# A fused attention and GeGLU kernel: a planner decides the order of work, a quarter of the softmax exponentials is computed on VectorE, and the softmax is normalised with queries on partitions

## The chip, the cores and the metric

The kernel runs on one core of one Trainium2 chip. The metric is the device time of one execution in microseconds, lower is better. Each kernel was run several times; a time "854.13 (853.46 to 855.33)" is the median and the range. A profile is one of these executions; its span is about 2 us shorter than the time of the same run.

Engines are named as in the profile: PE is TensorE's matmuls, PEld its weight loads, DVE is VectorE, ACT is ScalarE, POOL is GpSimd, SP is SyncE.

## The reference

```
x: 2048 tokens x 640;  H = 32 heads of Dh = 20;  Df = 1536          (bf16)
h  = x + Attention(layernorm(x))     # one k and one v head (20 wide) for all 32 query heads
     q = xn @ wq (2048 x 640),  k = xn @ wk,  v = xn @ wv (2048 x 20)
     p = softmax(q_h k^T / sqrt(20)),  o_h = p v,  concat(o_h) @ wo
h2 = h + FFN(layernorm(h))           # gelu(xn2 @ w_gate) * (xn2 @ w_up), then @ w_down
```

The heavy part is not a matmul. There are 32 x 2048 x 2048 scores, 134 million, and each needs an exponential. A matmul that makes scores contracts over only 20 numbers.

## The kernel before

Scores are made transposed, keys on partitions and 512 queries along the columns, so that the second matmul can sum over keys. Four heads are worked on at once: one *pack* is four score tiles of 128 keys x 512 queries, one per head, made by four matmuls on four row groups of TensorE. There are 512 packs. Each tile fills one PSUM bank. Six of the eight banks form three *pairs*; a pack takes two pairs, and ScalarE reads a pair in one instruction of 128x1024.

```python
def qk_fn(e, s):                       # L455: one pack of scores into two pairs of banks
    qc, g, kt = steps[s]
    pa, pb = pair_of_step[s]           # the third pair is left over from the pack before
    for half, pr in ((0, pa), (1, pb)):
        for rr in range(2):
            r = 2 * half + rr
            ins = e.matmul(bank(PAIRS[pr][rr]),
                kT4[32 * r:32 * r + 32, kt * P:(kt + 1) * P],
                qT[32 * r:32 * r + 32, qc % 2, g, :], start=True, stop=True, tile_position=(32 * r, 0))
    return ins

def exp_fn(e, s, half):                # L471: every exponential is ScalarE's, 128x1024 at a time
    ...
    return e.activation(PT[s % 2][:, half * 1024:(half + 1) * 1024], src, ACT.Exp, scale=SM_SCALE)

def pv_fn(e, s):                       # L477: weighted sums of v; a column of ones in v_ext gives the softmax's divisor
    for hl in range(4):
        ins = e.matmul(ps[32 * hl:32 * hl + 32, 6 * 512:7 * 512], v_ext[:, kt, :],
            PT[s % 2][:, hl * 512:(hl + 1) * 512], start=(kt == 0), stop=(kt == NKT - 1), ...)
```

After 16 key tiles the sums of four heads are copied out. The divisor lies in one row of each 32; a matmul with `bcast` spreads it over its block, and VectorE takes the reciprocal of the whole 128x512 tile:

```python
# piece_L, L516
plan.op("pe",  (lambda e: e.matmul(bank(7), bcast[:], opvT16[:, gi % 2, :], ...)), ...)
plan.op("dve", (lambda e: e.tensor_copy(rL_sb[:], bank(7))), ...)
plan.op("dve", (lambda e: e.reciprocal(rL_sb[:], rL_sb[:])), ...)        # L527: 128x512, 32 times
plan.op("dve", (lambda e: e.tensor_tensor(onT[...], opvT32[...], rL_sb[:], ALU.mult)), ...)
```

The GELU is built from a tanh (which shares ScalarE's table with exp: the trace before has one table load, at 0.7 us) and five steps on three engines: copy (DVE), square (POOL), `g_z` (DVE), tanh `g_th` (ACT), `g_hg` (DVE), `hhT` (DVE), for 48 tiles of 128x512. The FFN of the first three quarters of the tokens runs beside the exponentials; that of the last quarter runs after them. The order of the instructions on each engine is written by hand in the program.

The softmax here doesn't subtract the row's maximum and nothing guards it: scores larger than these inputs give would overflow.

## Time and profile before

The time is 1118.53 us in the runs given with the kernel (1117.71 to 1120.25).

| what | where it is read | value |
|---|---|---|
| head: first exponential | timeline | at 29.6 us |
| loop: first to last exponential | timeline | 985.0 us |
| tail: from the last exponential to the end | timeline | 102.7 us |
| ScalarE busy in the loop | busy time by window | 961.3 of 985.0 us |
| exponentials, busy | groups | 950.5 us, 0.928 us each |
| full-width reciprocals | groups | 107.3 us, 3.35 us each |

The page of the profile before: busy time of each engine, then two engines and the granted clock of TensorE in 40 slices of the span, each digit a share in tenths (for PEclk the share of full speed), then the start of the chain of work that ended last.

```profile
PE 760.8 (68%) x5424; PEld 204.0 (18%) x5508; DVE 457.8 (41%) x693; ACT 978.6 (88%) x1088; POOL 80.4 (7%) x104
...
ACT  0799999999899999999999999999999999993030
...
PEclk9799655555899999755999999985997699966998
...
ACT 74%; DVE 16%; PE 9%; issue 1%; DMA 1%; POOL 0%; another core or an unknown queue 0%
```

The groups of the kernel before: line, engine, operation, tiles, count, then busy time and the mean of one in ns, then the idle time before them and what ended most of it.

```profile
L475 ACT ACTIVATE scratch_a<-ps 128x1024 bf16<-128x1024 f32 x1024 | 950.5, 1132 | 24.2 <-PE ps L462 23.3
...
L527 DVE RECIPROCAL rL_sb<-rL_sb 128x512 f32<-128x512 f32 x32 | 107.3, 3353 | 1.1
```

Busy time of the kernel before in windows of the span (the loop, one stretch inside it, the tail); the columns are named in the first line.

```profile
core 0: us, PE busy (x) PEld busy (x) DVE busy (x) ACT busy (x) POOL busy (x), PEclk, DMA share, GB/s
29.60:1014.60 985.00, 685.02 (x5017) 170.51 (x5093) 378.44 (x525) 961.27 (x1060) 51.89 (x68) 0.81 0.05 13
150.00:275.00 125.00, 83.85 (x548) 15.50 (x548) 24.54 (x22) 125.00 (x137) 0.00 (x0) 0.50 0.00 1
1014.60:1117.30 102.70, 71.22 (x373) 31.66 (x381) 56.02 (x92) 14.63 (x25) 13.49 (x13) 0.89 0.07 20
```

Read together: ScalarE is at nine tenths or more in nearly every slice of the loop and waits 23.3 us in all for scores. Between 150 and 275 us TensorE runs at half its clock, and ScalarE does not lose a tenth of a microsecond by it. Neither TensorE nor VectorE is the limit. The last four slices of ScalarE's row (3, 0, 3, 0) are the tail.

The mean of one exponential in the groups (1132 ns) is longer than the 928 ns from one start to the next, because neighbouring instructions overlap in the record. Where instructions run back to back, count the busy time divided by the number, not the mean.

### The profile page before, as it was taken

What the parts mean: (1) busy time and instruction counts of PE and PEld (TensorE: products, weight loads), DVE (VectorE), ACT (ScalarE), POOL (GpSimd) and SP (SyncE); (2) the same over time, 40 slices, a digit from 0 to 9 for tenths busy, and PEclk for the clock granted to TensorE, in tenths of its full rate; (3) what the DMA queues carried; (4) which work ended last, traced back from release to release, by engine and by line L of the source; (5) the groups of instructions that cost most, each with busy time, mean ns of one, the idle gap of its engine ahead of it and who ended that gap; (6) DMA issues with size and microseconds to landing.
All of it is one profiled execution on the core that took longest, in us unless ns stands there. A gap on an engine that the chain in (4) does not pass through costs nothing.

```text
span 1117.3 us, 13050 instructions
## 1 busy us (share of the span) xinstructions
PE 760.8 (68%) x5424; PEld 204.0 (18%) x5508; DVE 457.8 (41%) x693; ACT 978.6 (88%) x1088; POOL 80.4 (7%) x104
## 2 busy tenths in 40 slices
PE   1677666666667776666777777767766766766866
PEld 0121111111121111111221111111221111112322
DVE  7433222211164656421224455642333356533573
ACT  0799999999899999999999999999999999993030
POOL 5200000000000111000000011100000011100130
PEclk9799655555899999755999999985997699966998
DMA  5460000000000000000000100000000000000100
GB/s 155 91 216 1 1 1 1 1 1 1 1 16 9 1 1 1 1 1 0 19 6 1 24 1 1 1 1 1 19 6 18 6 2 1 1 1 1 48 0 24
DMA packets 31772, 18.92 MB, mean 17 GB/s; under 512 B 23520, under 2 KB 30432, under 8 KB 31712
## 3 DMA queue, kind: packets, MB, share of 16 engines
q1 hardware_dynamic: 31712, 18.08, 5.9%
q8 instruction: 43, 0.70, 0.3%
q14 instruction: 17, 0.14, 0.0%
HBM read 10.21 MB, written 2.62 MB: 11 GB/s over the span
## 4 chain that ended last, share of the span: by engine, by line
ACT 74%; DVE 16%; PE 9%; issue 1%; DMA 1%; POOL 0%; another core or an unknown queue 0%
ACT scratch_a L475 72%; DVE rL_sb L527 4%; PE ps L778 2%; ACT g_th L719 2%; PE ps L672 2%; DVE g_z L713 2%; DVE hhT L733 1%; DVE g_hg L725 1%; PE ps L481 1%; PE ps L462 1%; DVE stats L277 1%; DVE stats L272 1%; PE ps L970 1%; DVE onT L531 1%; DVE xn_tmp L323 1%
## 5 line engine op out<-in xcount | busy, mean ns | idle before, releaser
L475 ACT ACTIVATE scratch_a<-ps 128x1024 bf16<-128x1024 f32 x1024 | 950.5, 1132 | 24.2 <-PE ps L462 23.3
L481 PE MATMUL ps<-scratch_a,v_ext 128*32 128x512 bf16 x2048 | 245.9, 470 | 192.9 <-ACT scratch_a L475 186.4
L462 PE MATMUL ps<-qT,kT 32*128 32x512 bf16 x2048 | 243.0, 464 | 83.6 <-ACT scratch_a L475 77.5
L481 PEld LDWEIGHTS ps<-scratch_a,v_ext 128*32 128x32 bf16 x2048 | 54.2, 95 | 382.4 <-ACT scratch_a L475 375.9
L509 DVE COPY opvT<-ps 128x512 f32<-128x512 f32 x32 | 22.1, 692 | 247.5 <-PE ps L481 247.5
L462 PEld LDWEIGHTS ps<-qT,kT 32*128 32x128 bf16 x2048 | 53.2, 94 | 313.6 <-ACT scratch_a L475 299.3
L527 DVE RECIPROCAL rL_sb<-rL_sb 128x512 f32<-128x512 f32 x32 | 107.3, 3353 | 1.1
L707 POOL TENSOR_TENSOR g_sq<-g_gs 128x512 bf16<-128x512 bf16 x48 | 53.3, 1111 | 372.1 <-DVE g_gs L700 332.5
L672 PE MATMUL ps<-xnT,wg_sb 128*128 128x512 bf16 x220 | 65.5, 401 | 15.3 <-DVE hhT L733 9.9
L672 PE MATMUL ps<-xnT,wu_sb 128*128 128x512 bf16 x228 | 66.2, 395 | 6.9 <-DVE g_gs L700 5.0
L778 PE MATMUL ps<-wd_sb,hhT 128*128 128x512 bf16 x185 | 53.6, 422 | 11.2 <-DVE hhT L733 7.2
L767 DVE CAST g_us<-ps 128x512 bf16<-128x512 f32 x36 | 24.9, 691 | 80.1 <-PE ps L672 79.7
L297 POOL TENSOR_TENSOR ln_den<-ln_ve,halfc 128x4 f32<-128x4 f32 x8 | 8.1, 1010 | 637.9 <-DVE ln_ve L295 622.6
L719 ACT ACTIVATE g_th<-g_z 128x512 bf16<-128x512 bf16 x48 | 34.6, 721 | 19.1 <-DVE g_z L713 19.1
L702 ACT ACTIVATE g_gs<-ps 128x512 bf16<-128x512 f32 x12 | 7.2, 597 | 48.5 <-PE ps L672 48.5
L525 DVE COPY rL_sb<-ps 128x512 f32<-128x512 f32 x32 | 22.0, 689 | 60.2 <-PE ps L481 53.3
L413 DVE CAST qT<-ps 128x512 bf16<-128x512 f32 x31 | 21.4, 689 | 56.6 <-PE ps L591 56.6
L700 DVE CAST g_gs<-ps 128x512 bf16<-128x512 f32 x36 | 24.8, 689 | 41.6 <-PE ps L672 41.6
L713 DVE SCALAR_TENSOR_TENSOR g_z<-g_sq,g_gs 128x512 bf16<-128x512 bf16 x48 | 39.6, 825 | 4.2 <-POOL g_sq L707 4.2
L725 DVE SCALAR_TENSOR_TENSOR g_hg<-g_th,g_gs 128x512 bf16<-128x512 bf16 x48 | 33.3, 695 | 10.9 <-ACT g_th L719 10.9
L733 DVE SCALAR_TENSOR_TENSOR hhT<-g_hg,g_us 128x512 bf16<-128x512 bf16 x36 | 31.4, 871 | 1.2
L616 PE MATMUL ps<-wo_pad,onT 128*128 128x512 bf16 x88 | 28.3, 397 | 4.9 <-DVE onT L531 3.6
(69 smaller groups left out, 362.4 us busy)
## 6 DMA issues: line engine op xcount, KB each, us to landing
xh_sb<-in_A_x_dram SPq DMA_DIRECT2D x4, 640.0 KB, 6.2
out_dram<-xh_sb SPq DMA_DIRECT2D x16, 160.0 KB, 1.8
wg_sb<-in_B_w_gate_dram SPq DMA_DIRECT2D x1, 1920.0 KB, 7.8
wu_sb<-in_B_w_up_dram SPq DMA_DIRECT2D x1, 1920.0 KB, 13.2
wd_sb<-in_B_w_down_dram SPq DMA_DIRECT2D x1, 1920.0 KB, 17.9
hhT<-in_A_wq_dram SPq DMA_DIRECT2D x1, 800.0 KB, 7.8
wo_pad<-in_A_wo_dram SPq DMA_DIRECT2D x32, 25.0 KB
xnT<-xn_tmp SPq DMA_TRANSPOSE x32, 2.6
```

The source lines that it names most:

```text
L462: ins = e.matmul(bank(PAIRS[pr][rr]), kT4[32 * r:32 * r + 32, kt * P:(kt + 1) * P], qT[32 * r:32 * r + 32, qc % 2, g, :], start=True, stop ...
L475: return e.activation(PT[s % 2][:, half * 1024:(half + 1) * 1024], src, ACT.Exp, scale=SM_SCALE)
L481: ins = e.matmul(ps[32 * hl:32 * hl + 32, 6 * 512:7 * 512], v_ext[:, kt, :], PT[s % 2][:, hl * 512:(hl + 1) * 512], start=(kt == 0), stop= ...
L527: plan.op("dve", (lambda e: e.reciprocal(rL_sb[:], rL_sb[:])), wait=[("Lcopy", gi)], mark=("recip", gi))
L616: ins = e.matmul(bank(7), onT[:, qc % 2, g, qt * P:(qt + 1) * P], wo_pad[:, g, 0:512], start=(g == 0), stop=(g == NG - 1))
L672: ins = e.matmul(bk, wsb[:, cc, fc * P:(fc + 1) * P], xnT[:, cc, tok], start=(cc == 0), stop=(cc == NC_D - 1))
L707: plan.op("pool", (lambda e: e.tensor_tensor(g_sq[:, s2(k), :], g_gs[:, s3(k), :], g_gs[:, s3(k), :], ALU.mult)), wait=[("gs", k)] + ([("z ...
L713: plan.op("dve", (lambda e: e.scalar_tensor_tensor(g_z[:, s2(k), :], g_sq[:, s2(k), :], GELU_K, g_gs[:, s3(k), :], ALU.add, ALU.mult)), wa ...
L719: plan.op("act", (lambda e: e.activation(g_th[:, s2(k), :], g_z[:, s2(k), :], ACT.Tanh, scale=GELU_C)), wait=[("z", k)] + ([("hg", kp)] if ...
L725: plan.op("dve", (lambda e: e.scalar_tensor_tensor(g_hg[:, s2(k), :], g_th[:, s2(k), :], 1.0, g_gs[:, s3(k), :], ALU.add, ALU.mult)), wait ...
L733: plan.op("dve", (lambda e: e.scalar_tensor_tensor(hhT[:, tc % 2, fc, :], g_hg[:, s2(k), :], 0.5, u_src, ALU.mult, ALU.mult)), wait=waits, ...
L778: ins = e.matmul(bk, hhT[:, tc % 2, fc, qt * P:(qt + 1) * P], wd_sb[:, fc, 0:512], start=(fc == 0), stop=(fc == NFC - 1))
```

## The change

The intent is to take work from ScalarE, and to fill the other engines with it.

**Chords.** Multiply a score by 128/ln 2 times the softmax scale, add a constant, and store it as a 16-bit integer; read the same bits as bf16. The integer part of the exponent lands in the exponent field and the rest in the mantissa, so the number read is a chord line of the exponential between two powers of two. One such line is too coarse. Adding 42 or 85 to the integer moves the corners of the chords by a third or two thirds of an octave; the change sums three such lines with weights. The sum would be about 3.12 times the exponential; the constant `CH_B` takes that factor out again, so that VectorE's tiles and ScalarE's can be added up together. The sum costs VectorE nothing: TensorE forms it, with three copies of `v_ext` scaled by the weights. The divisor comes from the same columns, so it carries the same approximation.

**Who takes a tile** is decided by a planner when the program is built. It steps the engines' clocks forward with estimated costs, and gives each engine, when it comes free, the next thing it can do. For every pack it picks how many of the four tiles VectorE takes.

**The normalisation** turns the sums back with four small transposing matmuls, so that a query's divisor is one number on its partition, and takes the reciprocal of 128x16 instead of 128x512.

**The GELU** becomes one ScalarE function, in place on up to 128x1536, at the price of table switches.

The diff, cut to its core (the original is a rewrite of most of the file):

```diff
+CH_SHIFT = (0, 42, 85)
+CH_W = (1.0, 0.79296875, 0.63671875)
+CH_NORM = 3.1233043861440573
 ...
+    CH_A = SM_SCALE * 128.0 / 0.6931471805599453
+    CH_B = (127.0 - math.log2(CH_NORM)) * 128.0
 ...
+    # issue_qk: how many tiles n of a pack does VectorE take?
+        for n, ca in ((0, 1810.0), (1, 1382.0), (2, 904.0), (3, 478.0), (4, 0.0)):
+            if n > nf or (n and state["npack"] < 4):
+                continue
+            m = max(A + ca, Dv + 900.0 * n)        # A, Dv: work that is queued on ScalarE, VectorE
+            if best is None or m < best[0] - 1.0:
+                best = (m, n)
+        n = best[1]
+        (_, a0, a1), (_, b0, b1) = gs[0], gs[1]    # two free pairs of banks
+        rr = [(k + i) % 4 for i in range(4)]
+        if n <= 2:
+            lay = [(rr[2], a0), (rr[3], a1), (rr[0], b0), (rr[1], b1)]
 ...
+        elif n == 1:
+            dve_q.append(tiles[rr[0]])
+            act_q.append(("S", [tiles[rr[1]]]))               # S: one tile, 128x512
+            act_q.append(("P", [tiles[rr[2]], tiles[rr[3]]])) # P: a pair, 128x1024
+        elif n == 2:
+            dve_q.append(tiles[rr[0]])
+            dve_q.append(tiles[rr[1]])
+            act_q.append(("P", [tiles[rr[2]], tiles[rr[3]]]))
 ...
+    # dve_decide: the pass from PSUM                                             (L1263)
+            op = plan.commit("dve", lambda e: e.tensor_scalar(pd[:, 0, s * 512:(s + 1) * 512],
+                     bank(b), CH_A, CH_B, ALU.mult, ALU.add), c_dve(512), L_DVE, ...)
+    # do_adds: the two shifted chords, up to four tiles at a time                (L1245)
+        for w in (1, 2):
+            op = plan.commit("dve", (lambda w, a: lambda e: e.tensor_scalar(
+                pd[:, w, a], pd[:, 0, a], float(CH_SHIFT[w]), None, ALU.add))(w, a), ...)
+    # issue_pv: one matmul per tile and chord                                     (L968)
+                ins = e.matmul(ps[32 * r:32 * r + 32, ...], v_ext[:, it["kt"], it["w"], :], it["ap"], ...)
 ...
-            plan.op("dve", (lambda e: e.reciprocal(rL_sb[:], rL_sb[:])), ...)                  # 128x512
+            dve(lambda e: e.reciprocal(rcp[:, sr, :]..., v5[:, :, :, Dh]), 200, ...)            # 128x16
 ...
-        plan.op("act", (lambda e: e.activation(g_th[...], g_z[...], ACT.Tanh, scale=GELU_C)), ...)
+            task(("act",), (lambda v: lambda e: e.activation(v, v, ACT.Gelu_apprx_tanh))(v), ...)
```

By the counts of the built kernel, ScalarE has 522 exponentials of 1024 columns and 484 of 512, and VectorE takes 520 of the 2048 tiles.

## The prediction

> **What bounds it now.** ScalarE. The timeline puts the first exponential at 29.6 us; its last idle stretch (41.7 us, ending at 1056.4) puts the last one at 1014.6. In that 985 us stretch ScalarE never stops: the groups view gives 1024 exponentials of 128x1024 in 950.5 us busy, so 0.928 us each back to back, and the other tanh fill the rest. The chain of waits agrees (ACT 74%, the exponentials 72%). TensorE is 68% busy but only follows: between 150 and 275 us its granted clock was 0.50 and ScalarE was still busy 125.0 of 125 us. VectorE is 41% busy, 107.3 us of it a full 128x512 reciprocal taken 32 times. Head 29.6 us, loop 985, tail 102.7.
>
> **What changes, by instruction counts of the built kernel.**
> - ScalarE: 522 exponentials of 1024 columns and 484 of 512 instead of 1024 of 1024. 522 x 0.928 = 484 us; a 512 one is 0.928 less 512/1.2 ns = 0.50 us (estimate; copies of 512 start 0.49 apart in the trace), so 484 x 0.50 = 242 us. 36 tanh of 512 in the loop become 12 in-place gelus of 1536 columns (about 1.35 us, 16 us) with 6 table switches. The Trainium skill, "ScalarE: Activation LUTs", "What ACT_TABLE_LOAD costs": 1.28 us plus a drain, 2.66 together; the trace's one load took 1.28. So 8 to 16 us. Loop sum about 755 us.
> - VectorE takes 520 score tiles (25.4%). Each: one PSUM pass at 0.60 us start to start (that interval in the trace for 512 columns from PSUM), 312 us; plus two SBUF adds, 1040 tile equivalents merged into 832 instructions. If these run at four elements per cycle ("VectorE: DVE Perf Modes", "What auto-detection actually checks"), 0.21 us for 512; the trace's 128x640 bf16 tensor_scalar starts 0.31 apart, which agrees. About 200 us. Added about 510; removed the 107 us reciprocal, copies to fp32, and most gelu arithmetic. VectorE sum about 690 us.
> - TensorE: weighted-sum matmuls grow from 2048 to 3088, because a chord tile is summed three times: 260 rounds of four, 56 us at full clock. Narrower q, down and wo matmuls add a little. Estimated stream 510 us at full clock plus mode changes.
> - Head: tiles of one, first score pack after one normalised tile: 13 us. Tail: the FFN of only four token tiles remains, but its last tile is a serial chain (two transposes at 2.6 us, wo, LN, gate, gelu, down, out): 60 us.
>
> **On the critical path.** All of ScalarE's saving, until something else binds. Floor 13 + 755 + 60 = 828 us. But three engines now run at 75 to 95% in a fixed order, with three pairs of PSUM banks between them: a late VectorE pass holds a pair, so the next score pack, so ScalarE. I expect ScalarE fed 93% of the loop: 755/0.93 = 812. 13 + 812 + 60 = **885 us**, 840 to 945 in 8 of 10. Faster by over 2%: 0.96; within 2%: 0.02; slower: 0.02.
>
> **What would show it.** Groups: exponentials about 727 us busy; first VectorE pass near 0.6 us, adds near 0.2 to 0.35. ScalarE idle in the loop 40 to 90 us, released by score matmuls. Granted clock above the 0.824 of before, for TensorE has more to do. First exponential before 16 us; tail 50 to 70. VectorE busy 75 to 85%.
>
> **What would make it wrong.** Adds on 16-bit integers running one or two elements per cycle (VectorE would then bind, over 850); TensorE at half clock for long stretches, where score plus 1.5 weighted-sum rounds plus projections exceed ScalarE's 1.42 us a pack; a plan whose latencies are too short, so that ScalarE waits over 15%; a tail longer than 75 us.

## The result, and the profile after

| | time, us | ratio to before |
|---|---|---|
| before, same rounds | 1118.24 (1117.71 to 1120.25) | 1 |
| after | 853.18 (850.82 to 855.34) | 0.7632 [0.7612, 0.7652] |
| after, measured again in other rounds (e5) | 853.59 (852.81 to 856.85) | 0.7637 [0.7619, 0.7655] |

A ratio here and below is the mean time of a kernel's runs over the mean of the runs of the kernel before in the same rounds, with a 95% interval; it is not quite the ratio of the medians.

The page of the profile after, the same lines as above:

```profile
PE 730.3 (86%) x6973; PEld 269.4 (32%) x6973; DVE 742.2 (87%) x1856; ACT 763.4 (90%) x1070; POOL 26.9 (3%) x60
...
ACT  0779999999999999999999999999999999999322
...
PEclk9969979996898999999999998999999999999999
...
ACT 66%; PE 20%; DVE 10%; DMA 3%; issue 1%; SPq 0%; DVEq 0%
```

The groups of the profile after; all exponentials of ScalarE are one group, L1263 is VectorE's pass from PSUM, L1245 the adds of the shifts.

```profile
L1212 ACT ACTIVATE pa<-ps 128x512 bf16<-128x512 f32 (+1 forms) x1006 | 722.1, 935 | 21.4 <-PE ps L880 20.7
L1263 DVE TENSOR_SCALAR pd<-ps 128x512 uint16<-128x512 f32 x520 | 355.2, 687 | 48.4 <-PE ps L880 40.7
...
L1245 DVE TENSOR_SCALAR pd<-pd 128x512 uint16<-128x512 uint16 (+2 forms) x832 | 230.2, 319 | 8.8
```

Busy time after, by window: the loop and the tail, columns as before.

```profile
24.50:793.00 768.50, 670.69 (x6355) 220.49 (x6355) 701.96 (x1726) 747.82 (x1027) 12.95 (x28) 0.95 0.09 21
793.00:851.30 58.30, 55.42 (x576) 45.19 (x574) 23.71 (x64) 13.13 (x38) 0.56 (x1) 1.00 0.13 30
```

The two spans differ by 1117.3 - 851.3 = 266 us. The three windows say where it came from.

| part | before | after | gain |
|---|---|---|---|
| head | 29.6 | 24.5 | 5.1 |
| loop | 985.0 | 768.5 | 216.5 |
| tail | 102.7 | 58.3 | 44.4 |

ScalarE is still the limit. It is busy 747.8 of the 768.5 us of the loop (97.3%), and the 20.7 us that it waits for scores are about the whole rest. What it does became less: 722.1 us of exponentials instead of 950.5. What is new is that VectorE (91% of the loop) and TensorE (87%) have become nearly as full, so the busy shares alone no longer tell which engine matters.

The tail changed in kind. These are pieces of the chain that ended last, in order of time (start, duration, what ran). First the kernel before, one of the twelve rounds of its last GELU:

```profile
1081.90 1.46 DVE g_z L713
...
1083.38 0.64 ACT g_th L719
...
1084.04 0.70 DVE g_hg L725
...
1084.77 0.69 DVE hhT L733
```

And the kernel after, where nearly the whole tail is one piece:

```profile
796.96 3.88 DMA onT<-onq
...
800.89 47.61 PE ps L455 x514
```

Before, VectorE and ScalarE hand a tile to each other in steps of 0.64 to 1.46 us; the twelve rounds take 38 us of the 102.7, and before them ScalarE had been idle for 41.7 us, from the last exponential to the first gate of the last FFN. After, 514 matmuls run without a break: TensorE is busy 55.4 of 58.3 us.

### The profile page after: what moved, and what is told of

It reads as the page before. It is cut to its first block, busy times and chain, and to the rows that moved or that the text cites. A ratio compares the mean times of both kernels' runs of the same rounds, so it can differ in the third digit from the quotient of the medians.

```text
span 851.3 us, 17702 instructions
## 1 busy us (share of the span) xinstructions
PE 730.3 (86%) x6973; PEld 269.4 (32%) x6973; DVE 742.2 (87%) x1856; ACT 763.4 (90%) x1070; POOL 26.9 (3%) x60
## 4 chain that ended last, share of the span: by engine, by line
ACT 66%; PE 20%; DVE 10%; DMA 3%; issue 1%; SPq 0%; DVEq 0%
ACT pa L1212 64%; PE ps L455 11%; PE ps L968 5%; PE ps L880 5%; DVE pd L1263 4%; DVE pd L1245 2%; ACT gbuf L732 1%; DMA xn1T<-xn_tmp 1%; DMA xh<-in_A_x_dram 1%; DVE stats L374 1%; DVE stats L367 1%; DMA onT<-onq 0%; DVE xn_tmp L435 0%; DVE xh L646 0%; ACT L1212 0%
## 5 line engine op out<-in xcount | busy, mean ns | idle before, releaser
L1212 ACT ACTIVATE pa<-ps 128x512 bf16<-128x512 f32 (+1 forms) x1006 | 722.1, 935 | 21.4 <-PE ps L880 20.7
L1263 DVE TENSOR_SCALAR pd<-ps 128x512 uint16<-128x512 f32 x520 | 355.2, 687 | 48.4 <-PE ps L880 40.7
L968 PE MATMUL ps<-pd,v_ext 128*32 128x512 bf16 x1560 | 280.3, 405 | 21.3 <-ACT pa L1212 14.1
L968 PE MATMUL ps<-pa,v_ext 128*32 128x512 bf16 x1528 | 272.2, 404 | 11.8 <-ACT pa L1212 8.0
L1245 DVE TENSOR_SCALAR pd<-pd 128x512 uint16<-128x512 uint16 (+2 forms) x832 | 230.2, 319 | 8.8
L968 PEld LDWEIGHTS ps<-pd,v_ext 128*32 128x32 bf16 x1560 | 67.2, 95 | 110.1 <-issue 47.9
L968 PEld LDWEIGHTS ps<-pa,v_ext 128*32 128x32 bf16 x1528 | 66.1, 94 | 92.4 <-issue 42.0
L455 PE MATMUL ps<-xn2T,wu_sb 128*128 128x512 bf16 (+2 forms) x360 | 69.0, 317 | 6.0 <-DVE gbuf L747 5.9
L455 PE MATMUL ps<-xn2T,wg_sb 128*128 128x512 bf16 (+2 forms) x360 | 68.1, 311 | 0.0
L455 PE MATMUL ps<-wd_sb,gbuf 128*128 128x320 bf16 x384 | 59.6, 300 | 0.0
```

What stands on the lines that cost most here:

```text
L455: return lambda e, b: e.matmul(o(b), l, r, start=st, stop=sp, **kw)
L968: ins = e.matmul(ps[32 * r:32 * r + 32, ab * 512:(ab + 1) * 512], v_ext[:, it["kt"], it["w"], :], it["ap"], start=st, stop=(j in ends), ti ...
L1212: op = plan.commit("act", lambda e: e.activation(dst, src, ACT.Exp, scale=SM_SCALE), cost, L_ACT, [("b", b0 + i) for i in range(n)], [("pa ...
L1245: op = plan.commit("dve", (lambda w, a: lambda e: e.tensor_scalar(pd[:, w, a], pd[:, 0, a], float(CH_SHIFT[w]), None, ALU.add))(w, a), k * ...
L1263: op = plan.commit("dve", lambda e: e.tensor_scalar(pd[:, 0, s * 512:(s + 1) * 512], bank(b), CH_A, CH_B, ALU.mult, ALU.add), c_dve(512), ...
```

## The experiments

Twelve runs were made, on several chips, one of them of the unchanged kernel again; the kernel before was run with each of them, and every ratio is against those runs. A profile's line numbers can be off by one to five between kernels, since an edit moves lines: L1211 to L1216 is the exponential, L879 to L884 the score matmul.

The theory after the result: **ScalarE's own work sets the loop, the chords took it away, and the fullness of VectorE and TensorE does not matter for the order that was built.** The rivals: the gain comes from the planner, or from the higher clock of TensorE (0.956 against 0.824), which both changed too; or VectorE or TensorE, at about 90%, now holds the loop.

### e1_no_chords: everything but the chords

```diff
-            if n > nf or (n and state["npack"] < 4):
+            if n > 0:
                 continue
```

> The changed kernel with every exponential left on ScalarE (the planner, the normalisation and the one-instruction gelu stay). Theory A (ScalarE sets the loop; the chords give most of the gain): loop of 1024 exponentials at 0.928 us plus about 17 us gelu and 13 us table loads, 980 to 1000 us, with a head of 24 and a tail of 58: 1062 to 1085 us, ScalarE busy over 97% of the loop, VectorE down to about 270 us busy. Rival (the planner's ordering and the cheaper normalisation give the gain, the chords only shift work): under 950 us.

Correct, 1069.09 us (1067.42 to 1073.53), ratio 0.9575 [0.9545, 0.9606]. The planner, the normalisation, the GELU, head and tail together are worth 1118.24 - 1069.09 = 49 us. The chords are worth the other 1069.09 - 853.18 = 216 us. The loop took 1012.5 us, with ScalarE busy 980.2 of them (97%), and the tail only 29.8: with a longer loop, more of the FFN fits beside it. So the chords gain 244 us in the loop and give 28.5 back in the tail. The loop and the tail of this run, columns as before:

```profile
23.50:1036.00 1012.50, 772.50 (x5729) 238.86 (x5729) 196.03 (x436) 980.15 (x1058) 12.30 (x27) 0.77 0.07 17
1036.00:1065.80 29.80, 16.46 (x162) 13.01 (x160) 8.84 (x26) 4.88 (x14) 0.56 (x1) 0.73 0.07 17
```

The granted clock was 0.771 here, lower than before the change, and ScalarE was still fed 97% of the time. So the higher clock does not explain the gain. Why the clock is higher after the change is not shown: in e1 TensorE was busier than in the kernel before (74% of the span against 68%) and was granted less. A smaller effect of the clock is not excluded: among the runs of one kernel, those with a higher clock are the shorter ones by some tenths of a per cent (850.8 at 0.962, 855.3 at 0.948), and no run shows which follows from which.

### e2_short_adds: VectorE's adds cut to one column, order kept

```diff
-                pd[:, w, a], pd[:, 0, a], float(CH_SHIFT[w]), None, ALU.add))(w, a), ...
+                pd[:, w, a.start:a.start + 1], pd[:, 0, a.start:a.start + 1], float(CH_SHIFT[w]), ...
...
-                                       "ap": pd16[:, w, s * 512:(s + 1) * 512], "free": fr})
+                                       "ap": pd16[:, 0, s * 512:(s + 1) * 512], "free": fr})
```

The planner is told nothing, so every engine runs the same instructions in the same order. The result is wrong (all three sums read the first chord; relative error 0.065).

> The changed kernel's own instruction order, with each of the 832 chord additions cut to one column (so each takes about 0.1 us in place of 0.28 and up) and the sums reading the first chord instead: a wrong result on purpose. VectorE loses 130 to 160 us of its 742 us busy; ScalarE's and TensorE's work is untouched. Theory A (ScalarE binds, VectorE only keeps up): 830 to 853 us, at most 2.5% faster, since ScalarE idles 21 us in the loop. Rival (VectorE, 94% busy in the loop, binds as much): 760 to 810 us.

854.13 us (853.46 to 855.33), ratio 0.7641 [0.7627, 0.7655]: no gain at all. The page of this run, then what two of its groups and its waits became (the last line is from the waits: engine, line, releaser, us in total, times, longest):

```profile
PE 730.0 (86%) x6973; PEld 268.8 (32%) x6973; DVE 618.3 (73%) x1856; ACT 763.2 (90%) x1070; POOL 26.2 (3%) x60
...
L1263 DVE TENSOR_SCALAR pd<-ps 128x512 uint16<-128x512 f32 x520 | 356.8, 690 | 168.5 <-PE ps L880 161.8
...
L1245 DVE TENSOR_SCALAR pd<-pd 128x1 uint16<-128x1 uint16 x832 | 87.1, 148 | 8.8
...
ACT pa L1212 <- PE ps L880: 22.0, 31, 3.6
```

VectorE was relieved of 742.2 - 618.3 = 124 us. All but 3 us of that turned up as VectorE waiting for score matmuls (40.7 became 161.8), and ScalarE's wait stayed at 22 us. An engine that is 87% busy was not in the way.

### e3_short_sums: TensorE's chord sums cut from 512 to 32 columns, order kept

```diff
-                ins = e.matmul(ps[32 * r:32 * r + 32, ab * 512:(ab + 1) * 512], ..., it["ap"], ...)
+                m = 512 if it["w"] == 0 else 32
+                ins = e.matmul(ps[32 * r:32 * r + 32, ab * 512:ab * 512 + m], ..., it["ap"][:, 0:m], ...)
```

Wrong too (relative error 0.25). Only the second and third chord's matmuls are cut: 1040, not the 1560 of which the expectation speaks.

> The changed kernel's own order, with the weighted-sum matmuls of all 1560 chord slices cut from 512 to 32 columns: a wrong result on purpose. TensorE loses about 70 us of streaming. Theory A: 835 to 853 us, within 2%. Rival (TensorE, 86% busy, paces the loop): 790 to 830 us. If neither this nor the shorter additions shorten it by more than 2.5%, the loop is ScalarE's.

853.17 us (852.00 to 856.33), ratio 0.7636 [0.7616, 0.7656]: no gain. ScalarE waited 21.2 us for scores, as before. How much work it took from TensorE is less sure than in e2, because the ends of matmuls are modelled: busy PE fell only from 730.3 to 714.1 us. The expectation had counted on 70 us.

So VectorE does not hold the loop: e2 shows it. For TensorE e3 is a weak test, and the stronger argument is the trace of the kernel after itself: ScalarE is idle for 20.7 us of the loop in all, so relieving TensorE alone could shorten the loop by no more than that. ScalarE's own work holds it.

### e4_wide_reciprocal: the old 128x512 reciprocal put back

```diff
-            dve(lambda e: e.reciprocal(rcp[...], v5[:, :, :, Dh]), 200, [("b", b)], [("rcp", sr)], 0.8, c1)
+            def c0(op):
+                dve(lambda e: e.reciprocal(rcp[...], v5[:, :, :, Dh]), 200, [("b", b)], [("rcp", sr)], 0.8, c1)
+            dve(lambda e: e.reciprocal(wide[:], bank(b)), 3353, [("b", b)], ["wide"], 0.8, c0)
```

The wide reciprocal's result is not used; it only costs its time, and the planner knows of it.

> The changed kernel with the old kernel's 128x512 reciprocal (32 times 3.35 us, 107 us) put back beside the small one, and told to the planner, which then leaves 460 tiles to VectorE instead of 520 and puts part of an FFN batch into the tail. Theory A: VectorE's time is now worth ScalarE's time, so it costs 30 to 70 us: 885 to 925 us. Rival (VectorE has the slack to take it, as before the change): under 865 us.

Correct, 935.00 us (931.19 to 939.22), ratio 0.8365 [0.8327, 0.8403]: 82 us slower, above what was expected. The 32 reciprocals took 107.1 us. The 78 us by which the profiled spans differ lie in three places. The planner gave VectorE 460 tiles instead of 520, so ScalarE's work in the loop rose from 747.8 to 771.7 us (+24). ScalarE was idle 50.2 us instead of 20.7 (+29.5), and the tail grew from 58.3 to 84.0 (+26), because more of the FFN was left for it (675 matmuls against 576). Only the first part is exponentials given back; why ScalarE was idle longer was not tested.

### b1_short_reciprocal: the same instruction in the kernel before

```diff
-            plan.op("dve", (lambda e: e.reciprocal(rL_sb[:], rL_sb[:])), ...)
+            plan.op("dve", (lambda e: e.reciprocal(rL_sb[:, 0:1], rL_sb[:, 0:1])), ...)
```

Wrong (garbage).

> The kernel before, with each of its 32 reciprocals of 128x512 cut to one column (wrong result on purpose): VectorE loses 105 us of its 458 us busy. Theory A (VectorE was off the path before; the new normalisation saves nothing by itself): within 1% of the kernel before. Rival (the normalisation holds bank 7 and with it the projections): 1060 to 1105 us.

1103.37 us (1102.06 to 1106.06), ratio 0.9859 [0.9844, 0.9874]. The same 107 us of VectorE are worth 15 us in the kernel before, against 82 in the kernel after. The two are not quite alike: here the order was kept and the work taken out, in e4 the planner made a new order with the work put in. The gain was slightly more than the 1% expected, and just inside the range of the rival (1060 to 1105 us), so that a small part of the normalisation was in the way before. The parts seen: ScalarE's wait for scores fell from 23.3 to 13.9 us, and its longest wait in the tail, for the last reciprocal among others, from 41.7 to 38.8.

So the normalisation saved little by itself. It was worth more beside the chords, where VectorE's time can be turned into ScalarE's: 24 of the 82 us of e4 are that exchange, the rest is waiting and tail.

### e5_after_again and e6_head_order: the head

The prediction had the first exponential before 16 us; it came at 24.54. GpSimd's instructions run in the order in which they are written. This is the timeline of GpSimd after (start, duration, line, operation, tiles, count, idle time before it and its releaser):

```profile
7.54 1.91 POOL L332 COPY wq_pad<-gbuf 128x400 bf16<-128x400 bf16 x4 [3.39 <-DMA gbuf<-in_A_wq_dram]
...
12.71 1.90 POOL L332 COPY wq_pad<-gbuf 128x400 bf16<-128x400 bf16 x4 [0.88 <-DMA gbuf<-in_A_wq_dram]
14.58 3.21 POOL L393 TENSOR_TENSOR ln_denb<-ln_veb,halfc 128x1 bf16<-128x1 bf16 x5
```

The last line is the square root of the first layer norm. Its input was there at 5.4 us, but it stands behind copies of the second half of `wq`, whose load lands at 12.7 us. In e6 those copies and other set-up work became tasks that the planner places, and the planned latencies of the loads were lengthened.

```diff
-        pool(lambda e: e.tensor_copy(o, i), 400, reads=[...], writes=[("wqp", g)])
+        task(("pool",), lambda e: e.tensor_copy(o, i), 500, L_POOL, [...], [("wqp", g)], 0)
...
-    load("act", wq_stage[:, :, HALF:D], ..., [("wqs", 1)], lat=4000)
+    load("act", wq_stage[:, :, HALF:D], ..., [("wqs", 1)], lat=10000)     # and five more loads
```

> The changed kernel unaltered, to be compared with the three others of this call in the same rounds: 850 to 856 us.

> The changed kernel with the head put in order: the query-weight copies and the second memset are planned as tasks on GpSimd instead of standing in its queue ahead of the layer norm's square root, and the input transfers are given longer planned latencies. Theory (the first square root starts at 14.6 us because GpSimd waits in order for the second weight transfer, which lands at 12.7): the first score matmul comes 6 to 10 us earlier and so does everything: 842 to 848 us. Rival (the head is bound by the input transfers themselves): within 3 us of the changed kernel.

e5, the unchanged kernel again: 853.59 us, ratio 0.7637. e6: correct, 850.54 us (843.80 to 852.29, six runs), ratio 0.7596 [0.7572, 0.7620]: about 3 us faster, with intervals that just touch, not the 5 to 11 that were expected. The edit did what it was meant to do:

```profile
6.31 1.07 POOL L392 TENSOR_TENSOR ln_denb<-ln_veb,halfc 128x1 bf16<-128x1 bf16 x2
```

The square root ran 8.3 us earlier and the first exponential at 17.99 us, 6.5 us earlier. But the last exponential ended at the same time, 792 against 793 us; the loop became 774.0 us instead of 768.5. Of these 5.5 us, 4.0 are more waiting (24.7 us idle instead of 20.7), among it gaps of 0.5 to 1.2 us between 24 and 30 us, when keys are still being made, and 1.4 are more work of ScalarE. Why it waits longer is not settled. So the rival had the size right (within 3 us), though not for its reason: the head did become shorter. The chain that leads to the first exponential in e6 also shows why 8.3 us gave only 6.5: the first transposing transfer took 5.9 us (8.05 to 13.94) against 2.5 in the kernel after.

### e7_two_chords and e8_two_chords_head: a cheaper chord sum

If ScalarE's work is all that counts, VectorE should take more tiles. Two chords instead of three take one add and one matmul away from each tile.

```diff
-CH_SHIFT = (0, 42, 85)
-CH_W = (1.0, 0.79296875, 0.63671875)
-CH_NORM = 3.1233043861440573
+CH_SHIFT = (0, 64)
+CH_W = (1.0, 0.70703125)
+CH_NORM = 2.0812
...
-            m = max(A + ca, Dv + 900.0 * n)
+            m = max(A + ca, Dv + 750.0 * n)
...
-        for w in (1, 2):
+        for w in (1,):
```

VectorE got 687 tiles, ScalarE 517 exponentials of 1024 and 327 of 512. e8 adds the head of e6.

> The changed kernel with sums of two chord lines in place of three (rows shifted by half an octave): one addition a tile instead of two, one weighted-sum pass fewer. Told to the planner, which gives VectorE 687 tiles instead of 520; ScalarE keeps 517 exponentials of 1024 and 327 of 512. Theory A (ScalarE's work sets the loop, so what VectorE saves pays only by being turned into more tiles): ScalarE's loop sum is about 690 us, so head 24, loop 710, tail 58: 785 to 805 us, result correct with a somewhat larger error. Rival (VectorE's tile pass from PSUM, not the additions, is its limit): 815 us or more.

> Both of the two changes above. If they are independent: the two-chord time less 6 to 10 us, 777 to 799 us. This would be the fastest.

Both are correct, and both are slower than the kernel after: 890.54 us (887.78 to 890.98), ratio 0.7957 [0.7940, 0.7975], and 882.56 us (882.35 to 883.55), ratio 0.7893 [0.7877, 0.7908]. The expectations of 785 to 805 and of 777 to 799 failed. ScalarE's work did shrink nearly as calculated, to 699.1 us in the loop of e7 (about 690 were expected). But the loop took 805.0 us. The wait of ScalarE in e8:

```profile
ACT pa L1211 <- PE ps L879: 108.6, 164, 5.8
```

and a piece of its timeline:

```profile
302.18 2.43 ACT L1211 ACTIVATE pa<-ps 128x512 bf16<-128x512 f32 x3 [0.50 <-PE ps L879]
305.11 5.73 ACT L1211 ACTIVATE pa<-ps 128x512 bf16<-128x512 f32 x8 [0.50 <-PE ps L879]
```

The rival here said that VectorE's passes would be the limit. It got the size right and the mechanism wrong: VectorE waits for score matmuls too (58.6 us in e7). Both engines wait, so it is neither's capacity.

### e9_alternate: three chords, but two tiles of every second pack

With two chords the planner gives VectorE two tiles of about 180 packs. With three it nearly always gives one: 484 of the 512 packs leave ScalarE a single tile. When VectorE takes two, they lie in one pair of banks, and ScalarE has just one pair to read. The new theory: **after that one piece ScalarE has nothing, because the next pack needs two free pairs and gets the second only when this pack's first pair is done with.** To test it with the kernel after, three chords and hardly fewer tiles:

```diff
-        n = best[1]
+        n = min(2, nf) if state["npack"] >= 4 and state["npack"] % 2 else 0
```

> The changed kernel (three chords) with VectorE's tiles dealt two to every second score pack instead of about one to each: 508 tiles in all against 520, ScalarE with 770 exponentials of 1024 and none of 512, so its sum is about 8 us smaller, and VectorE's additions are wider and cheaper. Theory R (what slowed the two-chord kernel is the round trip: a pack of two VectorE tiles puts both in one pair of banks and leaves ScalarE one pair alone, so after it ScalarE has nothing until a bank pair has come free and the next score matmuls are through, about 0.5 us): 254 such packs cost 60 to 130 us of ScalarE idle, 900 to 970 us. Rival (only the sums of work of the engines count): 840 to 860 us.

Correct, 1003.52 us (1000.77 to 1003.80), ratio 0.8965 [0.8950, 0.8979]: 150 us slower than the kernel after, with 508 tiles against 520. That is more than expected: ScalarE's idle time in the loop grew by 134 us (155.2 against 20.7), and its busy time by 32 (779.5 against 747.8), though its exponentials are fewer by count. The timeline of ScalarE in e9, and the wait:

```profile
900.62 2.85 ACT L1212 ACTIVATE pa<-ps 128x1024 bf16<-128x1024 f32 x3 [0.50 <-PE ps L880]
903.97 2.85 ACT L1212 ACTIVATE pa<-ps 128x1024 bf16<-128x1024 f32 x3 [0.50 <-PE ps L880]
907.33 2.86 ACT L1212 ACTIVATE pa<-ps 128x1024 bf16<-128x1024 f32 x3 [0.50 <-PE ps L880]
...
ACT pa L1212 <- PE ps L880: 153.2, 243, 5.3
```

Two packs give three pieces, then 0.50 us of nothing, again and again: 3.36 us for two packs. The other engines around one gap, in the same run:

```profile
902.14 1.29 DVE L1263 TENSOR_SCALAR pd<-ps 128x512 uint16<-128x512 f32 x2
...
903.53 0.40 PE L880 MATMUL ps<-qT,kT 32*128 32x512 bf16 x4
...
903.97 1.02 ACT L1212 ACTIVATE pa<-ps 128x1024 bf16<-128x1024 f32 x1 [0.50 <-PE ps L880]
```

VectorE's two passes end at 903.43 and ScalarE's third piece at 903.47. Only then is a second pair free. The matmuls start at 903.53, take 0.40, and ScalarE goes on at 903.97. In this gap TensorE had other matmuls to do until 903.48; in the gap before it stood idle, waiting for ScalarE, and the gap was the same 0.50 us. VectorE waited as well (189.3 us on score matmuls). The gap is a round trip through TensorE, not a lack of capacity.

### e11_alternate_split: e9 with only the layout of the tiles changed

```diff
-        if n <= 2:
+        if n == 2:
+            lay = [(rr[0], a0), (rr[2], a1), (rr[1], b0), (rr[3], b1)]
+        elif n < 2:
             lay = [(rr[2], a0), (rr[3], a1), (rr[0], b0), (rr[1], b1)]
...
-            act_q.append(("P", [tiles[rr[2]], tiles[rr[3]]]))
+            act_q.append(("S", [tiles[rr[2]]]))
+            act_q.append(("S", [tiles[rr[3]]]))
```

Now each of the two pairs holds one tile of each engine. The first pair comes free while ScalarE still has its second tile to do. The price is two instructions of 512 in place of one of 1024, an estimated 0.07 us of ScalarE (2 x 0.50 - 0.928).

> The alternating kernel of e9 (three chords, two VectorE tiles in every second pack, 508 in all), with one edit: in those packs each pair of banks gets one VectorE tile and one ScalarE tile, so ScalarE has two pieces of 512 in place of one of 1024. Its sum of ScalarE work grows by about 18 us. Theory R (the round trip after a pack whose ScalarE tiles lie in one pair): ScalarE's idle falls from 153 us to under 60, 860 to 910 us. Rival (dealing unevenly is itself the loss: VectorE gets its work in lumps): 970 us or more.

Correct, 909.01 us (905.92 to 914.93), ratio 0.8130 [0.8089, 0.8171], inside the expected range. The same tiles go to the same engines, and the layout alone took 94.5 us away. The wait of ScalarE, to be held against the last line of e9's timeline fence:

```profile
ACT pa L1215 <- PE ps L882: 31.7, 64, 4.6
```

This settles the larger part of what made e9 slow. For e7 and e8, where the same gap of 0.50 us stands in the timeline, e10 is the test.

What remains to the kernel after, 56 us: ScalarE was busy 30 us longer in the loop (777.7) and idle 31 us more. Of those 30 us only about 6 follow from the counts and the two start-to-start times (516 x 0.928 + 508 x 0.50 = 733 us against 727). The groups of e11, with the two sizes kept apart, tell where the rest is:

```profile
L1215 ACT ACTIVATE pa<-ps 128x1024 bf16<-128x1024 f32 x516 | 501.5, 1021 | 47.4 <-PE ps L882 27.5 <-PE ps L971 0.2
L1215 ACT ACTIVATE pa<-ps 128x512 bf16<-128x512 f32 x508 | 277.8, 609 | 4.5 <-PE ps L882 4.2
```

In all 253 places where a 512 piece is followed by a 1024 piece ScalarE stops, for 0.10 us in the median and 45 us in all (the view of waits leaves out stops under 0.15 us). A piece before a stop is not overlapped by the next one: it counts with its whole 0.61 us, and not with the 0.48 that lie between two starts. So one cause, a short stop in every second pack, makes up both the idle time and most of the 24 us. Why it stops there is not settled.

### e10_split_pairs: two chords, the head, and the split layout

```diff
 # e8, and:
-        for n, ca in (..., (2, 904.0), ...):
+        for n, ca in (..., (2, 956.0), ...):        # the two single tiles cost more
+        if n == 2:
+            lay = [(rr[0], a0), (rr[2], a1), (rr[1], b0), (rr[3], b1)]
...
+            act_q.append(("S", [tiles[rr[2]]]))
+            act_q.append(("S", [tiles[rr[3]]]))
```

> The two-chord kernel with the ordered head, but with the four tiles of a two-VectorE-tile pack laid one VectorE and one ScalarE tile to each pair of banks, so that ScalarE has two pieces in two pairs; the planner then gives VectorE 624 tiles, ScalarE 403 exponentials of 1024 and 618 of 512 (683 us). Theory R: ScalarE is fed again, idle under 50 us in the loop, 795 to 830 us: faster than the changed kernel and than the two-chord ones before it (883). Rival (two chords cost through TensorE's slower clock or VectorE's pass from PSUM): 850 us or more.

Correct, 848.48 us (842.46 to 851.77, five runs), ratio 0.7573 [0.7547, 0.7599]. It is 34 us faster than e8, which is what the layout should do, though the planner also dealt out fewer tiles to VectorE. It is the fastest of all kernels, though by little: 0.8% under the kernel after (0.7637 [0.7619, 0.7655], measured on another chip), and its interval overlaps that of e6 (0.7596 [0.7572, 0.7620]). The expected 795 to 830 was missed; the rival had said 850 or more.

The profiled run is the fastest of its five, 6 us below their median, and has the highest clock of them, so its parts sum to less than the median. In it the loop was 754.5 us and ScalarE busy 719.4 (95%); the head took 19.3 and the tail 66.6. In waits over 0.15 us, ScalarE waited for scores no longer than in the kernel after:

```profile
ACT pa L1214 <- PE ps L881: 20.7, 38, 5.3
```

The expectation knew the counts: the planner gives VectorE 624 tiles, not 687, and leaves ScalarE 403 instructions of 1024 and 618 of 512, because two single tiles cost it more. ScalarE's idle time came as expected, too (35.1 us in the loop, under 50). What came out larger than expected or than in the kernel after are the exponentials (694.9 us against 683) and the tail (66.6 us against 58.3). Against the kernel after, the two-chord sum gains 28 us of ScalarE in the loop, and gives 14 back in idle time and 8 in the tail.

## Why the prediction was right or wrong

The prediction said 885 us, 840 to 945; the result was 853.2. It was inside the range, and the direction and its reason were right: ScalarE limits, and what is taken from it in the loop comes off the time. That the number is as near as it is owes something to luck, as the terms show. Its terms:

| term | predicted | measured |
|---|---|---|
| head | 13 | 24.5 |
| ScalarE's work in the loop | 755 | 747.8 |
| share of the loop in which ScalarE is fed | 93% | 97.3% |
| loop | 812 | 768.5 |
| tail | 60 | 58.3 |

The measured terms sum to the span, 851.3. Two errors had opposite signs: the head was 11.5 us too short, the loop 43.5 us too long.

- **"I expect ScalarE fed 93% of the loop"**: this is the mis-sized term; it was 97.3%, 36 of the 43.5 us. The argument was that three engines at 75 to 95% would disturb each other through the three pairs of banks. That chain exists: it is the 0.50 us gap of e9, where ScalarE idled over 150 us. But it depends on how tiles are dealt out to pairs, not on how full the engines are (e2 took 124 us from VectorE and gained nothing; e11 changed the layout alone and gained 94.5 us). The planner with three chords mostly gives VectorE one tile of a pack, the case in which ScalarE has two pieces and no gap. ScalarE idle was predicted at 40 to 90 us; it was 20.7.
- **ScalarE's work** was right within 1%: exponentials 722.1 us against 727, twelve GELUs 16.8 against 16, and table switches at the low end. The Trainium skill, "ScalarE: Activation LUTs", "What ACT_TABLE_LOAD costs", gives a load of about 1283 ns and a drain of about 1380. The trace has the 1283 ns, and no stretch for a drain on either side:

```profile
308.39 1.28 ACT L732 ACT_TABLE_LOAD   x1
309.68 5.60 ACT L732 ACTIVATE gbuf<-gbuf 128x1536 bf16<-128x1536 bf16 x4
315.29 1.28 ACT L1212 ACT_TABLE_LOAD   x1
316.59 3.35 ACT L1212 ACTIVATE pa<-ps 128x512 bf16<-128x512 f32 x4
```

- **VectorE** did its passes 0.60 us apart where two follow each other, as predicted (two of them take 1.29 us in e9's timeline); but their records, 0.69 us long and mostly not next to another pass, add up to 355.2 us and not 312. The adds took 230.2 us against 200. The prediction's 0.21 us for an add was an estimate, worked out from a mode of four elements per cycle. The Trainium skill, "VectorE: DVE Perf Modes", "What auto-detection actually checks", says when the engine takes it: all tensors 16-bit with unit step, and a single source and the destination in SBUF. The adds fulfil this, and the trace agrees: 512 columns took 285 ns and 1024 took 422, so 137 ns for 512 more, about 3.7 per ns, where VectorE's copies from PSUM, 417 ns for 256 columns and 680 for 512, get 0.97.

```profile
L1245 DVE TENSOR_SCALAR pd<-pd 128x512 uint16<-128x512 uint16 x650 | 157.8, 285 | 6.1
L1245 DVE TENSOR_SCALAR pd<-pd 128x1024 uint16<-128x1024 uint16 x166 | 63.1, 422 | 2.7
```

VectorE's busy sum was 742 us (87%), not 690 (75 to 85%).
- **TensorE** was granted 0.956 of its clock, above the 0.824 before, as predicted; why is not shown (see e1).
- **"Head: tiles of one, first score pack after one normalised tile: 13 us"** failed. The step overlooked GpSimd, whose order put the square root behind the copies of a later load (14.58 instead of 6.31 us in e6). That is 6.5 of the 11.5 us; with it mended, the first exponential still came at 18.0. And what e6 shows was not foreseen: mending the head by 6.5 us shortens the time by about 3 only.
- **"Tail ... its last tile is a serial chain ... 60 us"**: the number was right by luck, for the reason was wrong. There is a short serial chain at its start, but 47.6 us are one unbroken stream of matmuls, among them the down projection of an earlier batch that did not fit into the loop.

What was not settled: why e6 waits longer in the loop; why e11 still stops in every second pack; how much of e3's cut really reached TensorE; and whether the small spread of the times among runs of one kernel follows the clock or causes it.

## What to carry to other kernels

Ask which engine bounds the loop, and price every other engine's work by what it lets you take from that one: the same 107 us of VectorE reciprocals were worth 15 us before VectorE could take exponentials and 82 after (24 of them as ScalarE's work, the rest as waiting and tail). A busy share near 90% proves no limit; shorten the work with the order kept, as in e2, see in the trace that it did become shorter, and see if the time moves. When two engines share the tiles of one pair of PSUM banks, look at the round trip from the last reader through the refilling matmul and back (0.50 us here): deal the tiles so that a pair comes free while the bounding engine still has a piece to do, and give a planner that term, for one that weighs loads alone will walk into it, as with the two chords.

## What the Trainium skill lacked or had wrong

- "ScalarE: Activation LUTs", "What ACT_TABLE_LOAD costs", has 2.66 us for a switch of tables, of which 1.38 are a drain. In the six switches of the loop after the change, the load took 1283 ns, began within 0.02 us of the end of the activation before it, and the next activation started within 0.02 us of its end. Counted from start to start, so with the overlap that is lost, a switch cost 1.4 to 1.6 us.
- The same page, "Rules for kernel authors", calls ScalarE the only option for `exp`. The kernel after approximated 25.4% of 134 million exponentials on VectorE and stayed correct; two chords, with 687 of 2048 tiles on VectorE, were correct as well.
- "Perfetto Trace Analysis", "Identifying the Most-Contended Engine", takes the occupancy of ScalarE and VectorE as the measure of the bottleneck. It found the right one before (ScalarE 88%), and after the change too, but by 90% against 87%; what it does not tell is that the second of the two was no limit at all: taking 124 us from VectorE changed nothing.
- No page that bears on this gives the cost of waiting for a pair of PSUM banks to be read, refilled and read again: 0.50 us of an idle reader, of which 0.40 are the four score matmuls and 0.04 to 0.06 the handing over on either side.
